# Linear attention with a SwiGLU gate on one core: the w_phi load laid out by partition, four weight folds ahead of x's transposes, and the first two tiles of x normalised one by one

## Chip, cores and metric

The kernel runs on one core of one Trainium2 chip. The metric is device time in microseconds, the median of three runs. The opening of the kernel, the first 70 us or so, is what the change edits; the rest stays as it is.

## What is computed

x is 2048 rows by 1024 columns. It is layer-normalised to xn. From xn comes a gate (SwiGLU with 3584 hidden columns, then a Silu) and an attention value s: 32 heads of width 32, whose queries and keys go through a small matrix of their head, w_phi, and a softmax of the result and of its negative.

```
xn = layernorm(x)
q, k, v = split(xn @ wqkv)                       # 32 heads, width 32
phi(a) = [softmax(a @ w_phi[h]), softmax(-a @ w_phi[h])]
o = phi(q) (phi(k)^T v) / (phi(q) sum(phi(k)) + 1e-6)
s = o @ wo
g = silu((silu(xn @ w1) * (xn @ w3)) @ w2)
out = x + s * g
```

## The kernel before

Products are made in a Strassen-like form: a 2 x 2 block product takes seven block products instead of eight, with sums of blocks as operands (A11, A12, S1, S2, S3, S4 and A22 of x; B11, B21, T1 to T4 and B22 of the weights). Each operand is split by `split` (L91 to L94) into a rounded high part (a cast on ScalarE, L93) and a remainder (a subtraction on VectorE, L94), and each block product takes three passes of TensorE over these parts (L627). w_phi is not multiplied with queries and keys; it is folded into the weights beforehand: `fold` (L244 to L249) multiplies a transposed block of wk or wq with `bd`, a block-diagonal matrix made of w_phi by GpSimd (L293 to L296). There are 32 folds; 22 are made in the opening by `first_folds` (L306 to L314), 10 later, one by one, beside the main loop. A fold loads `wr` (256 KB, L241), runs eight matmuls into a PSUM tile `pw` (L248), is copied back over `wr` by ScalarE (L312), and is stored to DRAM (L313). All loads and stores here go through SP's one queue.

Two sets of buffers matter. `wr` comes from a pool `work` of five buffers (tag "w"), which block 0's weight sum `t2` shares in the opening. The PSUM tiles `pt` of the transposes (`turn`, L216 to L220) and `pw` of the folds share three buffers (tag "tr"); each is emptied by a copy on ScalarE (L224 or L312).

The opening (L275 to L361): load w_phi (L276), tiles 0 to 3 of x, the weights of block 0 of w1 and w3 (`rw`, L257), four fold blocks (L241), tiles 4 to 7 of x, the weights of block 1. Tiles 0 to 3 give A11 and A12, tiles 4 to 7 A21 and A22. For a tile, `stats` (L192 to L196) makes mean and variance on VectorE; `rstd` (L198 to L209) makes the reciprocal root for a pair of tiles, one square root on ScalarE (L202) and five small operations on VectorE (L203 to L208); `norm` (L211 to L214) normalises the two halves of a tile in place. Then come the transposes, copies and splits of A11 for the four tiles, two folds, those of A12, the splits of two operands of block 1, the statistics of tiles 4 to 7, and three folds. Then each of tiles 4 to 7 is turned, the sums S1 to S4 are made by VectorE (`a_sums`, L227 to L237) and two folds follow each tile; the last three operands are split with three folds after each. GpSimd sums block 0's weights (`b_sums`, L129 and L130) before the first of these.

A scheduler orders the instructions of each engine in this part, by program order and by when it takes their inputs to be ready. The main loop's first four products, (block 0: A11, A12; block 1: A11, A12), may be mixed with the opening; from step 4 on the order of the five engines is the program's (L616), and 56 blocks of seven products follow, with side work hung on their steps. Later phases make keys and values, queries, w2, and the output.

Of the kernel before, what the change touches and what calls it, by code (L numbers as in the profile page):

```python
# [8 lines left out]
F = mybir.dt.float32  # L9
# [7 lines left out]
S, D, H, DH, FF = 2048, 1024, 32, 32, 3584  # L17
P = 128
# [3 lines left out]
G = 8  # L22
# [6 lines left out]
def tile_kernel(ctx: ExitStack, tc: tile.TileContext, x, wkT, wqT, wv, wphi, wo, w1, w3, w2, out):  # L29
    nc = tc.nc  # L30
    open_pools = {}

    def pool(name, bufs, **kw):

        open_pools[name] = tc.tile_pool(name=name, bufs=bufs, reuse_waits="tile", **kw)
        return open_pools[name].__enter__()
# [101 lines left out]
    small = pool("small", 2)  # L138
    work = pool("work", 5)
# [14 lines left out]
    def slot(m, j):  # L154
        name = f"op{m}" + (ANAMES if m < 2 else BNAMES)[j]
        j = HOMES[m][j]
        if j < 7:
            return big.tile([P, 2, 4, 512], R, name=name, tag=f"big{j}")
        return spare.tile([P, 2, 4, 512], R, name=name, tag=f"spare{j}")
# [12 lines left out]
    def quad(name, dt=R):  # L172
        return qp.tile([P, 2, 4, P], dt, name=name, tag="q")

    def blk(name):
        return xp.tile([P, 4, P], F, name=name, tag="x")

    def flat(t):
        return t.rearrange("p k t -> p (k t)")
# [7 lines left out]
    def load_x(t, halves):  # L187
        for h in range(2):
            nc.sync.dma_start(halves[h], x[t * P:(t + 1) * P, h * 512:(h + 1) * 512])
        return halves  # L190

    def stats(mv, j, xt):  # L192
        st = small.tile([P, 2, 6], F, name="st")
        for a in range(2):
            nc.vector.bn_stats(st[:, a, :], xt[a])
        nc.vector.bn_aggr(mv[:, j], st.rearrange("p a b -> p (a b)"))  # L196

    def rstd(mv):  # L198

        sd = small.tile([P, 4, 2], F, name="sd")  # L200
        var = mv[:, :, 1]
        nc.scalar.activation(sd[:, 0], var, AF.Sqrt, bias=eps_t)  # L202
        nc.vector.reciprocal(sd[:, 1], sd[:, 0])  # L203

        nc.vector.tensor_mul(sd[:, 2], sd[:, 1], sd[:, 1])
        nc.vector.scalar_tensor_tensor(sd[:, 3], var, EPS, sd[:, 2], op0=OP.add, op1=OP.mult)
        nc.vector.tensor_scalar(sd[:, 3], sd[:, 3], -0.5, 1.5, op0=OP.mult, op1=OP.add)
        nc.vector.tensor_mul(sd[:, 1], sd[:, 1], sd[:, 3])  # L208
        return sd  # L209

    def norm(mv, sd, j, xt):  # L211

        for a in range(2):
            nc.vector.tensor_scalar(xt[a], xt[a], mv[:, j, 0:1], sd[:, 1, j:j + 1], op0=OP.subtract, op1=OP.mult)  # L214

    def turn(half):  # L216
# [22 lines left out]
    def load_w(wT, dch, c, t=None):  # L239
        wr = blk("wr") if t is None else t  # L240
        nc.sync.dma_start(wr, wT[dch][:, 4 * c:4 * c + 4])  # L241
        return wr

    def fold(wr, c):  # L244

        pw = ps.tile([P, 4, P], F, name="pw", tag="tr", bufs=3)
        for g in range(4):
            nc.tensor.matmul(pw[:, g, :], wr[:, g], bd[:, 4 * c + g, :], start=True, stop=True)  # L248
        return pw  # L249

    folds = [(wkT, k, c, wk_d[c][k]) for c in range(2) for k in range(ND)]
    folds += [(wqT, k, c, wq_d[c][k]) for c in range(2) for k in range(ND)]

    def b_load(f, rw, n):

        a, h = {"B11": (0, 0), "B21": (0, 1), "B12": (1, 0), "B22": (1, 1)}[n]
        nc.sync.dma_start(rw[:, a, h], (w1, w3)[a][f][:, 4 * h:4 * h + 4].rearrange("p k n -> p (k n)"))  # L257
# [15 lines left out]


    phi_raw = flat(blk("phi")[:, :2]).rearrange("p (g f) -> p g f", f=DH)  # L275
    nc.sync.dma_start(phi_raw, wphi.rearrange("(g p) f -> p g f", p=P))  # L276
    ao, bo, bo1, xs = {n: slot(0, j) for j, n in enumerate(ANAMES)}, {}, {}, []
    rws = [rwp.tile([P, 2, 2, 512], F, name="rw", tag="rw") for _ in range(2)]
    for t in range(8):
        if t in (4, 5):  # L280
            xs.append(load_x(t, [flat(blk("xt")) for _ in range(2)]))
        else:
            r = quad("xt", F).rearrange("p u k t -> p u (k t)")
            xs.append(load_x(t, [r[:, 0], r[:, 1]]))
        if t == 3:
            for n in ("B11", "B22", "B12", "B21"):
                b_load(0, rws[0], n)
            early_w = [load_w(*folds[k][:3], work.tile([P, 4, P], F, name="wr", tag="w")) for k in range(4)]
    for n in ("B11", "B21", "B22", "B12"):
        b_load(1, rws[1], n)  # L290
    make_identity(nc, ident)
# [14 lines left out]
    def first_folds(n):  # L306
        nonlocal at_fold
        for _ in range(n):
            wT, k, c, d = folds[at_fold]
            wr = early_w.pop(0) if early_w else load_w(wT, k, c, work.tile([P, 4, P], F, name="wr", tag="w"))  # L310
            pw = fold(wr, c)
            nc.scalar.copy(wr, pw)  # L312
            nc.sync.dma_start(d, flat(wr))  # L313
            at_fold += 1  # L314

    mvs = [small.tile([P, 2, 2], F, name="mv", bufs=4) for _ in range(4)]
    raw = [{} for _ in range(4)]
    for t in range(4):
        stats(mvs[t // 2], t % 2, xs[t])
    for p in range(2):  # L320
        sd = rstd(mvs[p])
        for j in range(2):
            norm(mvs[p], sd, j, xs[2 * p + j])
    for q in range(4):
        raw[q]["A11"] = raw_x(turn(xs[q][0]))
        first_split("A11", q, raw[q]["A11"])
        if q == 1:
            next(b_gen)
    first_folds(2)
    for q in range(4):  # L330
        raw[q]["A12"] = raw_x(turn(xs[q][1]))
        first_split("A12", q, raw[q]["A12"])
# [4 lines left out]
        split(bo1[n][:, 0], bo1[n][:, 1], rws[1][:, 0, h].rearrange("p (k n) -> p k n", n=P))  # L337
    for q in range(4):
        stats(mvs[2 + q // 2], q % 2, xs[4 + q])
    first_folds(3)  # L340
    next(b_gen)
    for q in range(4):
        if q % 2 == 0:
            sd = rstd(mvs[2 + q // 2])
            for j in range(2):
                norm(mvs[2 + q // 2], sd, j, xs[4 + q + j])
        raw[q]["A21"] = raw_x(turn(xs[4 + q][0]))
        raw[q]["A22"] = raw_x(turn(xs[4 + q][1]))
        a_sums(raw[q], nc.vector)
        first_split("S2", q, raw[q]["S2"])  # L350
        first_split("S1", q, raw[q]["S1"])
        if q == 2:
            next(b_gen)
        first_folds(2)
# [58 lines left out]
    def side_x(i, s0):  # L413
# [9 lines left out]
        for j in range(2):  # L423
            at_ = room(at_ + 1, 1.6)
            at(at_, lambda j=j: stats(mv[0], j, xt[j]))
        at_ = room(at_ + 1, 1.0)
        at(at_, lambda: sd.append(rstd(mv[0])))
        for j in range(2):
            at_ = room(at_ + 1, 1.0)
            at(at_, lambda j=j: norm(mv[0], sd[0], j, xt[j]))  # L430
# [183 lines left out]
    for step, (k, an) in enumerate(seq):  # L614
        if step == 4:
            in_order(ENG.PE, ENG.Activation, ENG.DVE, ENG.Pool, ENG.SP)  # L616
        tb, f = divmod(k, NF)
# [475 lines left out]
    for r, new in enumerate(steps):  # L1093
# [31 lines left out]
        if 26 <= r < 34:  # L1125
            c, a = (r - 26) // 4, (r - 26) % 4
            nc.sync.dma_start(zr_d[32 * a:32 * a + 32, c], z_d[:, c, a].rearrange("o j s f -> o (j s f)").to_broadcast([32, 256]))
        if 8 <= r < 24:
            c, j, s = (r - 8) // 8, (r - 8) // 2 % 4, r % 2
# [64 lines left out]
    halves = [(b, a, c) for b in range(NB) for a in range(2) for c in range(2)]  # L1194
# [121 lines left out]
```

## Time and profile before

| | |
|---|---|
| median of three runs | 2379.27 us (2379.09 to 2381.4) |
| the profiled execution | 2381.26 us |
| its span | 2379.0 us |
| TensorE, VectorE, ScalarE, GpSimd busy | 98%, 75%, 36%, 32% |
| first transposes on TensorE | 13.65 us |
| last fold of the opening on TensorE | 70.02 us |

In the profile, PE is TensorE, PEld its weight loads, DVE VectorE, ACT ScalarE, POOL GpSimd and SP the engine that issues DMAs. A timeline row has a start in us, a duration in us, the engine, the line, the operation, output and inputs by their names with shapes, a count of instructions that were merged, and in brackets how long the engine had been idle before and what ended that. A windows row has the stretch and its length, then the busy time of PE, PEld, DVE, ACT and POOL with counts of instructions, the clock that TensorE was granted (1.00 is full), the busy share of the DMA engines, and GB/s. A row of the chain has a start, a duration and what the chain went through. A row of a group has a line, what it does and its count, then the busy time in us and the mean in ns, then the idle time before it and its cause. SPq is SP issuing a DMA.

### The profile page before, as it was taken

Reading aid. Unit: us, or ns where it says so; the run is one execution under the profiler, and the core shown is the slowest. Engines: PE = TensorE matmul, PEld = TensorE weight load, DVE = VectorE, ACT = ScalarE, POOL = GpSimd, SP = SyncE. Lnnn points to the kernel's source line nnn. Section 1 sums busy time; section 2 is a strip of 40 time slices with the busy share of each in tenths; the row PEclk is TensorE's granted clock in tenths of the full one; section 3 lists DMA queues with packets and bytes.
Section 4 is the critical chain, followed back from the end, with each engine's and each line's share of the span. In section 5 each row is a group of like instructions: output and inputs, shape, how many; then the busy total and the mean of one; then the engine's idle time right before and its main releaser. Section 6 shows DMA issues by size and latency. Waiting matters only on the chain.

```text
span 2379.0 us, 35819 instructions
## 1 busy us (share of the span) xinstructions
PE 2339.5 (98%) x13298; PEld 1923.9 (81%) x13298; DVE 1773.7 (75%) x2511; ACT 856.1 (36%) x1506; POOL 762.1 (32%) x569
## 2 busy tenths in 40 slices
PE   6999999999999999999999999999999999999999
PEld 5788888888888888888888787887888888887777
DVE  8567788775688878884575565787678788888993
ACT  6445544443345544453221111234422222242010
POOL 1333555552355555552000000230011111115872
PEclk9999999999999999999999999999999999999999
DMA  7667789877887787776998867998434443277653
GB/s 262 200 218 238 232 288 312 288 246 230 260 272 257 250 280 274 262 268 232 364 345 334 321 215 292 348 352 295 152 123 163 177 182 135 99 274 285 229 190 121
DMA packets 319406, 586.83 MB, mean 247 GB/s; under 512 B 25600, under 2 KB 158208, under 8 KB 316544
## 3 DMA queue, kind: packets, MB, share of 16 engines
q1 hardware_dynamic: 304448, 569.87, 69.3%
q10 hardware_dynamic: 14784, 14.68, 1.8%
q8 instruction: 105, 1.72, 0.3%
q14 instruction: 69, 0.57, 0.1%
HBM read 379.19 MB, written 205.79 MB: 246 GB/s over the span
## 4 chain that ended last, share of the span: by engine, by line
PE 90%; DVE 4%; DMA 3%; issue 1%; ACT 1%; POOL 0%; SPq 0%; ACTq 0%; POOLq 0%; DVEq 0%
PE bankb L627 25%; PE bankc L627 12%; PE bankb L1074 11%; PE bankb L679 10%; PE pm L1190 7%; PE banka L627 6%; PE bankc L1074 6%; PE bankc L679 5%; PE banka L1074 3%; PE banka L679 2%; PE po L1048 1%; PE pkv L665 1%; PE pw L248 1%; DMA hr<-h_d 1%; DMA e_d<-eq 0%
## 5 line engine op out<-in xcount | busy, mean ns | idle before, releaser
L94 DVE TENSOR_TENSOR bo<-rw,bo 128x512 fp32r<-128x512 f32 x336 | 311.7, 928 | 151.5 <-ACT bo L93 148.5
L1084 POOL TENSOR_TENSOR acc<-acc,u 128x512 f32<-128x512 f32 x48 | 64.4, 1342 | 455.5 <-ACT u L1083 440.8
L93 ACT CAST bo<-rw 128x512 fp32r<-128x512 f32 x336 | 201.1, 617 | 4.0 <-DMA w_d0T<-w2o 2.0
L1074 PE MATMUL bankb<-bo,as 128*128 128x512 f32 x816 | 201.1, 389 | 0.4 <-DVE acc L1086 0.4
L1074 PEld LDWEIGHTS bankb<-bo,as 128*128 128x128 f32 x816 | 153.1, 188 | 32.6 <-DVE acc L1086 0.8
L1190 PE MATMUL pm<-wos,oT 128*128 128x512 f32 x720 | 168.7, 393 | 3.6 <-DVE gx L1209 3.6
L627 PE MATMUL bankb<-op0A,bo 128*128 128x512 f32 x672 | 164.0, 391 | 0.0
L1190 PEld LDWEIGHTS pm<-wos,oT 128*128 128x128 f32 x720 | 135.6, 189 | 34.9 <-DVE gx L1209 4.0
L627 PE MATMUL bankb<-op0S,bo 128*128 128x512 f32 x672 | 163.0, 391 | 0.0
L627 PE MATMUL bankc<-op0S,bo 128*128 128x512 f32 x672 | 162.9, 391 | 0.0
L627 PE MATMUL bankc<-op1S,bo 128*128 128x512 f32 x672 | 161.5, 389 | 1.2 <-ACT bo L93 1.2
L627 PE MATMUL bankb<-op1A,bo 128*128 128x512 f32 x672 | 161.4, 389 | 0.0
L627 PE MATMUL bankb<-op1S,bo 128*128 128x512 f32 x672 | 161.4, 389 | 0.0
L627 PEld LDWEIGHTS bankc<-op1S,bo 128*128 128x128 f32 x672 | 126.0, 188 | 27.7 <-ACT bo L93 1.6
L1074 PE MATMUL bankc<-bo,as 128*128 128x512 f32 x576 | 146.6, 389 | 1.1 <-ACT as L93 0.7
L627 PEld LDWEIGHTS bankb<-op1S,bo 128*128 128x128 f32 x672 | 126.1, 188 | 26.2
L627 PEld LDWEIGHTS bankb<-op1A,bo 128*128 128x128 f32 x672 | 126.1, 188 | 26.2
L627 PEld LDWEIGHTS bankc<-op0S,bo 128*128 128x128 f32 x672 | 125.5, 188 | 25.7
L627 PEld LDWEIGHTS bankb<-op0A,bo 128*128 128x128 f32 x672 | 125.4, 188 | 25.7 <-DVE op0A L94 0.2
L627 PEld LDWEIGHTS bankb<-op0S,bo 128*128 128x128 f32 x672 | 125.4, 188 | 25.6
L1074 PEld LDWEIGHTS bankc<-bo,as 128*128 128x128 f32 x576 | 108.0, 188 | 24.3 <-ACT as L93 1.1
L129 POOL TENSOR_TENSOR rw<-rw 128x512 f32<-128x512 f32 x56 | 82.5, 1474 | 135.3 <-DMA rw<-in_w 119.2
(245 smaller groups left out, 4723.1 us busy)
## 6 DMA issues: line engine op xcount, KB each, us to landing
rw<-in_w SPq DMA_DIRECT2D x224, 256.0 KB, 3.5
hr<-h_d SPq DMA_DIRECT2D x56, 512.0 KB, 3.9
xoS<-xo_d0S SPq DMA_DIRECT2D x48, 512.0 KB, 8.7
xoS<-xo_d1S SPq DMA_DIRECT2D x48, 512.0 KB, 7.0
xoA<-xo_d0A SPq DMA_DIRECT2D x36, 512.0 KB, 7.8
xoA<-xo_d1A SPq DMA_DIRECT2D x36, 512.0 KB, 6.1
e<-e_d SPq DMA_DIRECT2D x32, 512.0 KB, 6.1
h_d<-h SPq DMA_DIRECT2D x56, 256.0 KB, 4.3
```

The costliest lines, as they stand in the source:

```text
L93: nc.scalar.copy(hi, src)
L94: (by or nc.vector).tensor_sub(lo, src, hi.bitcast(F))
L129: nc.gpsimd.tensor_sub(b12, b22, b12)
L248: nc.tensor.matmul(pw[:, g, :], wr[:, g], bd[:, 4 * c + g, :], start=True, stop=True)
L627: nc.tensor.matmul(bank, bt[:, w, kk], aos[tb][an][:, u, kk], start=an in ("A11", "A12", "S1") and n == 0, stop=LAST[b] == an and n == 11, ...
L665: nc.tensor.matmul(pkv[sl, m], e[:, m // 4, (m % 4) * P + 32 * h:(m % 4) * P + 32 * h + 32], v[:, 4 * (m % 4) + h], start=first and m == 0 ...
L679: nc.tensor.matmul(bank[b], xo[an][:, u, k], wb[bn][:, w, k], start=an in ("A11", "A12", "S1") and n == 0, stop=LAST[b] == an and n == 11, ...
L1048: nc.tensor.matmul(po[a][32 * j:32 * j + 32, 256 * c:256 * c + 256], kvt[sl, c, j, s], ets[c, j // 2][sl, 2 * (j % 2) + s].rearrange("p t ...
L1074: nc.tensor.matmul(bank[b], t[:, u, pos + k], bos[kb, bn, k][:, w], start=first and n == 0, stop=LAST[b] == an and n == 5, skip_group_chec ...
L1084: nc.gpsimd.tensor_add(c, c, u)
L1190: nc.tensor.matmul(p, oT[a][k // 4][:, u, k % 4], wos[c, 4 * (k % 2) + k // 2][:, w], start=n == 0, stop=n == 23)
```

## The change

w_phi is handed over in the layout of the SBUF tile, so that each partition reads one run of 1 KB; before, it read eight runs of 128 B. The four fold blocks that are loaded early are loaded ahead of block 0's weights. Tiles 0 and 1 of x are normalised one at a time, each with its own rstd, so there are three rstds for the first four tiles instead of two. Tiles 2 and 3 share one, and their first halves are normalised before their second halves. Four folds stand right behind tiles 0 and 1, ahead of the other tiles' statistics and of all transposes; the two folds between A11 and A12 are gone, and one stands where three stood. The opening still makes 22 folds.

```diff
-        sd = small.tile([P, 4, 2], F, name="sd")
+        sd = small.tile([P, 4, 2], F, name="sd", bufs=4)[:, :, :mv.shape[1]]
...
-    def norm(mv, sd, j, xt):
-
-        for a in range(2):
+    def norm(mv, sd, j, xt, *halves):
+
+        for a in halves or range(2):
             nc.vector.tensor_scalar(xt[a], xt[a], mv[:, j, 0:1], sd[:, 1, j:j + 1], op0=OP.subtract, op1=OP.mult)
...
-    nc.sync.dma_start(phi_raw, wphi.rearrange("(g p) f -> p g f", p=P))
+    nc.sync.dma_start(phi_raw.rearrange("p g f -> p (g f)"), wphi)
...
         if t == 3:
+            early_w = [load_w(*folds[k][:3], work.tile([P, 4, P], F, name="wr", tag="w")) for k in range(4)]
             for n in ("B11", "B22", "B12", "B21"):
                 b_load(0, rws[0], n)
-            early_w = [load_w(*folds[k][:3], work.tile([P, 4, P], F, name="wr", tag="w")) for k in range(4)]
...
-    for t in range(4):
-        stats(mvs[t // 2], t % 2, xs[t])
-    for p in range(2):
-        sd = rstd(mvs[p])
-        for j in range(2):
-            norm(mvs[p], sd, j, xs[2 * p + j])
+    for t in range(2):
+        stats(mvs[0], t, xs[t])
+        one = mvs[0][:, t:t + 1]
+        norm(one, rstd(one), 0, xs[t])
+    first_folds(4)
+    for t in range(2):
+        stats(mvs[1], t, xs[2 + t])
+    sd = rstd(mvs[1])
+    for a in range(2):
+        for t in range(2):
+            norm(mvs[1], sd, t, xs[2 + t], a)
...
-    first_folds(2)
     for q in range(4):
         raw[q]["A12"] = raw_x(turn(xs[q][1]))
...
-    first_folds(3)
+    first_folds(1)
...
-        "wphi": np.asarray(A_w_phi).reshape(H * DH, DH),
+        "wphi": np.asarray(A_w_phi).reshape(G, P, DH).transpose(1, 0, 2).reshape(P, G * DH),
```

## Prediction

> **What bounds the kernel now.** The page comes first: TensorE is busy nearly all of the span, and the chain that ended last is 90% TensorE.
>
> ```profile
> span 2379.0 us, 35819 instructions
> PE 2339.5 (98%) x13298; PEld 1923.9 (81%) x13298; DVE 1773.7 (75%) x2511; ACT 856.1 (36%) x1506; POOL 762.1 (32%) x569
> PE 90%; DVE 4%; DMA 3%; issue 1%; ACT 1%; POOL 0%; SPq 0%; ACTq 0%; POOLq 0%; DVEq 0%
> ```
>
> So a change to the opening can only win time in which TensorE does nothing there, and what it wins stays won if TensorE is dense afterwards. The windows view gives the opening by stage (busy time of each engine in ten microseconds).
>
> ```profile
> 0.00:10.00 10.00, 0.00 (x0) 0.00 (x0) 3.51 (x8) 1.58 (x2) 3.17 (x11) 1.00 0.77 251
> 10.00:20.00 10.00, 3.92 (x16) 2.88 (x17) 9.69 (x25) 3.07 (x7) 2.59 (x2) 1.00 1.04 390
> 20.00:30.00 10.00, 10.00 (x61) 9.26 (x60) 10.00 (x20) 8.82 (x18) 4.60 (x3) 1.00 0.59 212
> 30.00:40.00 10.00, 9.90 (x61) 8.19 (x60) 9.63 (x27) 9.12 (x19) 0.00 (x0) 1.00 0.63 210
> 40.00:50.00 10.00, 9.10 (x70) 8.01 (x68) 10.00 (x18) 9.11 (x19) 0.00 (x0) 1.00 0.69 236
> 50.00:60.00 10.00, 7.55 (x49) 5.85 (x47) 7.55 (x13) 8.73 (x17) 0.00 (x0) 1.00 0.87 269
> 60.00:70.00 10.00, 8.07 (x49) 6.54 (x50) 7.49 (x12) 5.15 (x10) 4.17 (x3) 1.00 0.86 277
> ```
>
> TensorE idles 16.1 us of the first 20, then 0.1, 0.9, 2.45 and 1.93 us per stage: 21.5 us in all. But from 10 to 50 VectorE is full and from 20 to 50 ScalarE is at nine tenths, so emptying TensorE there need not bring the end forward. The chain in order of time says what held which stretch.
>
> ```profile
> 2.33 5.71 DMA xt<-in_x
> ...
> 46.71 3.88 DMA wr<-in_wkT
> ...
> 55.36 3.14 DMA wk_d<-wr
> ...
> 65.19 4.70 DMA wr<-in_wqT
> ...
> 71.15 1.16 PE bankc L627 x5
> ```
>
> First the loads of x, then VectorE, and from about 43 us the folds: load, fold, copy, store, and only then is the buffer free for the next load. TensorE runs dense from 71.15. The question is how much earlier that moment comes.
>
> **Part 1: w_phi by partition.** The old view reads runs of 32 floats; the new one reads one run of 1 KB per partition.
>
> ```profile
> 2.00:3.40 1.40, 0.00 (x0) 0.00 (x0) 0.00 (x0) 0.01 (x1) 0.22 (x2) 1.00 1.04 221
> 8.10:10.00 1.90, 0.00 (x0) 0.00 (x0) 1.87 (x4) 0.30 (x1) 0.00 (x0) 1.00 1.05 402
> ```
>
> The DMA engines are as busy in the first stretch (share 1.04) as in the second (1.05), yet move 221 GB/s against 402: 0.31 MB where 0.56 MB would have gone, that is 0.25 MB, or 0.6 us at 402. The loads of x queue behind it on SP's one queue. Bounds: nothing, if SP's pace of issuing them is what counts, to the 1.4 us of the stretch. I take 0.6.
>
> **Part 2: the order of the loads.** SP issues in program order here.
>
> ```profile
> 1.24 3.89 SPq L189 DMA_DIRECT2D xt<-in_x  x8
> 5.17 3.85 SPq L257 DMA_DIRECT2D rw<-in_w  x4
> 9.30 2.31 SPq L241 DMA_DIRECT2D wr<-in_wkT  x4
> ...
> 24.88 1.95 SPq L241 DMA_DIRECT2D wr<-in_wkT  x2
> ...
> 42.94 0.33 SPq L241 DMA_DIRECT2D wr<-in_wkT  x1
> ```
>
> The four fold loads go from 9.30 to 5.17, block 0's weights behind them, so that GpSimd's sums of these weights come later by the 2.31 us that four issues took. Nobody waits for the sums soon: in the program the first use of these weights, the split of B11, stands behind the second tile's transposes, and those of the first tile run at 13.65 (row below). The cost is nothing but a collision, priced below.
>
> **Part 3: the first two tiles one by one.** VectorE's work up to the eighth norm, row by row.
>
> ```profile
> 4.71 1.34 DVE L195 BATCH_NORM_STATS2 st<-xt 128x6 f32<-128x512 f32 x2 [3.84 <-DMA xt<-in_x]
> 8.06 1.34 DVE L195 BATCH_NORM_STATS2 st<-xt 128x6 f32<-128x512 f32 x2 [1.77 <-DMA xt<-in_x]
> 9.56 1.23 DVE L195 BATCH_NORM_STATS2 st<-xt 128x6 f32<-128x512 f32 x2
> 12.73 0.29 ACT L202 ACTIVATE sd<-mv,consts 128x2 f32<-128x2 f32 x1 [2.76 <-DVE sd L207]
> 12.96 3.82 DVE L214 TENSOR_SCALAR xt<-xt,mv,sd 128x512 f32<-128x512 f32 x4
> 13.37 1.27 POOL L129 TENSOR_TENSOR rw<-rw 128x512 f32<-128x512 f32 x1 [8.33 <-DMA rw<-in_w]
> 13.65 1.09 PE L219 MATMUL pt<-ident,xt 128*128 128x128 f32 x4 [13.65 <-DVE xt L214]
> 14.72 1.32 POOL L130 TENSOR_TENSOR t<-rw 128x512 f32<-128x512 f32 x1
> 16.70 0.15 DVE L203 RECIPROCAL sd<-sd 128x2 f32<-128x2 f32 x1
> 17.69 1.92 DVE L214 TENSOR_SCALAR xt<-xt,mv,sd 128x512 f32<-128x512 f32 x4
> ```
>
> Before, the eight norms are done at 17.69 + 1.92 = 19.61, after a hole of 1.77 us in which VectorE waits for the second tile. Prices: a tile's statistics 1.50 (8.06 to 9.56), an rstd 0.99 (16.70 to 17.69), a norm of half a tile 0.48 (1.92 over four), the wait for ScalarE's square root about 0.4 (an estimate: the 0.29 of its row and the handing over). After, from x's landing at 4.71 - 0.6 = 4.1: 4 x 1.50 + 3 x 0.99 (one more than before) + 8 x 0.48 + 0.4 = 13.2, hence 17.3. The second tile is wanted at 4.1 + 1.50 + 0.4 + 0.99 + 0.96 = 7.95 and lands at 8.06 - 0.6 = 7.46: the hole is filled. The 0.99 of the added rstd has that hole as its cover; without it, it is lost in full. The waits for the other two square roots can be covered by other tiles' statistics; if not, they add up to 0.8.
>
> Then the collision. Four norms took 3.82 us while GpSimd ran L129 and L130, and 1.92 us without it: 1.90 us. After, these two sums start at about 13.37 + 2.31 - 0.6 = 15.1 and last 2.7 us, and the last four norms would run from 15.4 to 17.3: again wholly beside them. I take the full 1.90: eight norms done at 19.2, a gain of 0.4 us. Bounds: -0.4 (collision and both waits) to 2.3 (neither). The Trainium skill, SBUF — State Buffer, Who interferes with whom, speaks against the change at this place: such a VectorE operation and a GpSimd operation exclude each other for a whole instruction, so that four separate norms can be stopped each time. By that rule the time lost is as before; had the trace shown no slowing, the eight norms would be done at 17.3.
>
> **Part 4: four folds first.** The next rows are what the folds cost and where they stand.
>
> ```profile
> L312 ACT COPY wr<-pw 128x512 f32<-128x512 f32 x22 | 12.9, 592 | 9.6 <-PE pw L248 9.6
> ```
>
> ```profile
> 32.40 0.50 ACT L202 ACTIVATE sd<-mv,consts 128x2 f32<-128x2 f32 x2
> 35.08 0.69 DVE L571 TENSOR_TENSOR h<-banka,h 128x512 f32<-128x512 f32 x1
> 35.67 2.82 DVE L214 TENSOR_SCALAR xt<-xt,mv,sd 128x512 f32<-128x512 f32 x6
> 36.01 1.28 ACT L572 ACT_TABLE_LOAD   x1
> 36.36 1.08 PE L219 MATMUL pt<-ident,xt 128*128 128x128 f32 x8
> 37.28 1.06 PE L248 MATMUL pw<-bd,wr 128*128 128x128 f32 x8
> 37.84 1.05 ACT L224 COPY xf<-pt 128x512 f32<-128x512 f32 x2
> ```
>
> A fold is eight matmuls, 1.06 us, and a copy of 0.59 us. Four of them, 4.2 us of TensorE and 2.4 us of ScalarE, leave the stretch 20 to 32 us for the empty one before 14. Who waits for it: the transposes stand behind these folds on TensorE. Issued at 5.17, with the 3.85 us that four issues then took and the 5.71 us from issue to landing of the chain's first row, less 0.6, the last one lands at about 9.0 + 5.7 - 0.6 = 14.1; the first transposes then start at about 15 instead of 13.65. By then two tiles are normalised and their four halves follow without a gap, and VectorE, which is the one that is full, has statistics and norms until 19: this costs nothing, at most 1.4 us if a split of A11 is what VectorE lacks.
>
> What does the lead bring? The folds after these four keep their places in the program: one ahead of the second group's transposes, two behind each tile of it, then three after each of the last operands. In the trace TensorE ran transposes and folds in program order throughout. Sixth fold: loaded with the pair issued at 24.88 (over at 26.83), in place some 4 us later (the load at 46.71 took 3.88), but run at 37.28, right behind the transposes of 36.36, which wait for the norms of 35.67. It lay ready for over 6 us. So the sixth and later folds move only as those norms do, by VectorE's 0.4 us, and the buffers' rounds with them: from 42.94 to 65.19 twelve loads, 2.02 us apart, five buffers, 10.1 us a round, in loads and stores that the change does not touch.
>
> Beyond the 0.4 us: at 36.36 ScalarE is late. The first four transposes are over near 36.9, but their copy runs at 37.84, behind a table load and a Silu. With 2.4 us of copies gone ahead of it, up to 0.9 us is won here; I take 0.9, since ScalarE is at nine tenths from 20 on. After it, VectorE waits 2.45 us between 50 and 60, mostly for ScalarE; what can be won there lies between 0 and 2.45, and I take 0.7, near the lower end, since in that stage ScalarE waits for folds (9.6 us in the row of L312).
>
> **Sum.** 0.4 + 0.9 + 0.7 = 2.0 us less. The profiled execution took 2381.26 us (span 2379.0 and 2.3 around it), so 2379.3 for it; the median of the runs is 2379.27, 2.0 below the profiled one, hence **2377.3**. Differences under 0.2%, 4.8 us, a measurement of this kernel can hardly tell from none.
>
> **Rivals.** *The folds keep their lead.* If the scheduler lets the sixth to eighth folds, whose buffers are then loaded well before 30 us, run ahead of the second group's transposes, the rounds start three folds earlier: 3 x 2.02 = 6.1 us, 2373.2. For it: TensorE waits at 50 to 70 for folds; ScalarE has 9.6 us of such waits. Against it: the sixth fold that lay ready. Chance 0.25.
>
> *The square roots fall behind the Silu.* Before, both square roots of the second group (32.40) stand ahead of the first Silu, so one table load (36.01, 1.28 us) is enough. With the folds off TensorE, block 0's second product can be ready before 32.40 rather than just before the add at 35.08; a Silu scheduled then makes ScalarE change tables twice more: 2.6 us in a stretch where it has no room, and VectorE's norms of 35.67 wait for it. From the point where that product is done more than 2.7 us earlier than now it decides; the four folds are 4.2 us of TensorE. It takes the 0.9 and 0.7 too: 2379.3 - 0.4 + 2.6 = 2381.5. Chance 0.12.
>
> *Nothing comes through.* The wr loads land late, the transposes start after 15 us, the collision and both square roots are paid (-0.4), and the rounds of the folds take what is left: 2379.3. Chance 0.13.
>
> **The numbers.** The forecast holds 0.50; its own range is 2375.0 (the terms at 2.3, 0.9 and 1.1) to 2379.7 (-0.4 and nothing else). For 8 in 10 the range reaches to the first rival and most of the second: 2371.5 to 2381.0. Faster by over 0.2%: the first rival and a little of the forecast's tail, 0.27; slower by over 0.2%: only the second rival with its waits doubled, 0.06; the rest, 0.67, lies between.
>
> **What would show it.** Right: x's first statistics near 4.1; the four folds on TensorE before any transpose; the eighth norm near 19 with norms slowed beside L129 and L130; the second group's first transposes near 36, the sixth fold right behind them; the first dense bank group near 69 instead of 71.15. Wrong: folds six to eight ahead of the transposes and dense work from 65; or more than two table loads on ScalarE before 55 us; or an idle VectorE between 10 and 30.

## The result, and the profile after

The changed kernel takes 2404.1 us (median of 4 runs, 2403.37 to 2406.54); the kernel before, in the same comparison, 2379.49 us (2379.09 to 2381.4). The ratio is 1.0104, 95% interval 1.0092 to 1.0116: 24.6 us slower, where 2.0 us less was forecast and the range ended at 2381.0. The profiled execution took 2406.54 us. Its page begins:

```profile
span 2404.5 us, 35834 instructions
PE 2363.2 (98%) x13298; PEld 1926.0 (80%) x13298; DVE 1770.0 (74%) x2516; ACT 857.4 (36%) x1507; POOL 760.4 (32%) x569
```

The span is 25.5 us longer, with the same 13298 matmuls; and TensorE's busy time is 23.7 us longer. A loss by waiting would show as idle time. This one shows mostly as matmuls that take longer, so the first question is which. The view of one line's instructions gives for each shape the count, the duration in ns (smallest, median, largest), and when the first and the last started. First the kernel before:

```profile
L627 PE MATMUL bankb<-op0A,bo x672: 387/389/499, 24.5 to 613.7; 128*128 128x512 f32 x168
L627 PE MATMUL bankb<-op1S,bo x672: 389/389/389, 608.4 to 1134.7; 128*128 128x512 f32 x168
L627 PE MATMUL banka<-op1A,bo x336: 389/389/389, 603.0 to 1121.1; 128*128 128x512 f32 x168
L679 PE MATMUL bankb<-op2T,xoS x192: 389/389/497, 1145.8 to 1299.7; 128*128 128x512 f32 x192
L1074 PE MATMUL bankb<-bo,as x816: 387/389/497, 1634.8 to 2174.4; 128*128 128x512 f32 x164
```

Then the changed kernel, whose lines stand four further down:

```profile
L631 PE MATMUL bankb<-op0A,bo x672: 387/389/497, 23.4 to 621.1; 128*128 128x512 f32 x168
L631 PE MATMUL bankb<-op1S,bo x672: 388/389/499, 615.8 to 1147.3; 128*128 128x512 f32 x168
L631 PE MATMUL banka<-op1A,bo x336: 394/394/394, 608.7 to 1133.6; 128*128 128x512 f32 x168
L683 PE MATMUL bankb<-op2T,xoS x192: 388/394/501, 1158.4 to 1313.8; 128*128 128x512 f32 x192
L683 PE MATMUL bankb<-op4T,xoS x192: 388/389/467, 1495.5 to 1641.1; 128*128 128x512 f32 x192
L1078 PE MATMUL bankb<-bo,as x816: 387/394/398, 1649.7 to 2197.8; 128*128 128x512 f32 x164
```

Read the starts first. The last fold of the opening runs 4.7 us late (74.72 against 70.02, rows below), and the first products with operands op1, near 600, 5.7 us (608.7 against 603.0 for banka). By 1650 it is 14.9 us (1649.7 against 1634.8), at the last product of that group 23.4 us. So two losses stand one behind the other, and the larger is nowhere near the edited code.

Now the durations of the 128x512 matmuls. Most take 389 ns as before, but all 336 with banka and op1A take 394, and so does the median of op2T's and of the last phase's. They do not share a phase, for op1S runs in the same one at 389. They share a place. The program lays its pools into a partition of SBUF from two ends: the small tiles, the five `wr` buffers, the weight operands `bo` and seven large operand slots from the left, and from the right the raw weights and the x blocks; the place of the x blocks is later taken by two more operand slots, and then by tiles of the late phases. Where the program's text names the place, the slow matmuls have one operand in each end (A11 and A12 of op1 lie in the right-hand slots); op0's, op1S's and op4's operands lie all in the left end and stay at 389. One group of 96 does not fit (bankb from op3T and xoA, both in the left end): its median is 393 here and 389 in e2 below.

A matmul's duration is not yet its price, since the next one starts before it ends: twelve of 389 ns would add up to 4.7 us, and they take 2.88. What counts is the time of such a row of twelve, first before, then after:

```profile
602.99 2.88 PE L627 MATMUL banka<-op1A,bo 128*128 128x512 f32 x12
```

```profile
608.65 2.96 PE L631 MATMUL banka<-op1A,bo 128*128 128x512 f32 x12
```

That is 0.08 us for twelve, 6.7 ns for each. Counted over the whole trace, 3389 of the 128x512 matmuls take 392 to 399 ns in the changed kernel and 294 before. The 3095 more, at 6.7 ns, come to 20.7 us.

What moved the ends against each other is two words of the first line in the diff: `sd` got bufs=4 in place of 2. An `sd` is 8 floats per partition, 32 bytes; two more push everything behind it in the left end up by 64 bytes, and nothing in the right end.

The opening itself, in the timeline of the changed kernel:

```profile
4.19 0.69 DVE L195 BATCH_NORM_STATS2 st<-xt 128x6 f32<-128x512 f32 x1 [3.33 <-DMA xt<-in_x]
11.03 6.68 PE L248 MATMUL pw<-bd,wr 128*128 128x128 f32 x32 [11.03 <-DMA wr<-in_wkT]
14.42 3.82 DVE L214 TENSOR_SCALAR xt<-xt,mv,sd 128x512 f32<-128x512 f32 x4
14.96 1.59 POOL L129 TENSOR_TENSOR rw<-rw 128x512 f32<-128x512 f32 x1 [10.34 <-DMA rw<-in_w]
16.62 1.33 POOL L130 TENSOR_TENSOR t<-rw 128x512 f32<-128x512 f32 x1
17.55 2.47 PE L219 MATMUL pt<-ident,xt 128*128 128x128 f32 x20
...
37.99 1.92 DVE L214 TENSOR_SCALAR xt<-xt,mv,sd 128x512 f32<-128x512 f32 x4
39.17 1.04 PE L219 MATMUL pt<-ident,xt 128*128 128x128 f32 x8
40.05 1.95 PE L248 MATMUL pw<-bd,wr 128*128 128x128 f32 x16
...
59.93 1.13 PE L248 MATMUL pw<-bd,wr 128*128 128x128 f32 x8 [2.81 <-DMA wr<-in_wkT]
63.70 2.05 PE L248 MATMUL pw<-bd,wr 128*128 128x128 f32 x8 [2.64 <-DMA wr<-in_wqT]
...
74.72 1.13 PE L248 MATMUL pw<-bd,wr 128*128 128x128 f32 x8 [0.26 <-DMA wr<-in_wqT]
```

It starts as forecast. x's first statistics run at 4.19, four folds come before any transpose, and the eighth norm ends at 14.42 + 3.82 = 18.24 instead of 19.61. Then the lead is lost: the second group's norms run at 37.99, where they ran at 35.67; TensorE waits 2.81 and 2.64 us for the loads of two folds near 60; and the last fold runs at 74.72 instead of 70.02. Near 60 SP issues in bunches: three loads from 50.89, three stores from 54.55, and no load again until 60.52, where before it issued them singly, mostly by turns. One row stands out: the eight matmuls at 63.70 take 2.05 us, those at 59.93 take 1.13. By the view of the line in these stretches one matmul takes 421 ns there and 275 ns here:

```profile
L248 PE MATMUL pw<-bd,wr x28: 344/421/553, 11.0 to 16.9; 128*128 128x128 f32 x28
L248 PE MATMUL pw<-bd,wr x8: 275/275/347, 59.9 to 60.8; 128*128 128x128 f32 x8
L248 PE MATMUL pw<-bd,wr x8: 421/421/552, 63.7 to 65.3; 128*128 128x128 f32 x8
```

The first of the three rows is that of the four folds at the front; they, too, ran at 421. So did the first folds of the kernel before, whose row is:

```profile
L248 PE MATMUL pw<-bd,wr x16: 421/421/421, 20.2 to 23.4; 128*128 128x128 f32 x16
```

The windows view of the changed kernel says what happened at 63.70 (the column behind POOL's is the granted clock):

```profile
30.00:40.00 10.00, 9.37 (x42) 7.81 (x43) 8.71 (x25) 5.92 (x12) 0.03 (x1) 0.83 0.46 150
...
60.00:70.00 10.00, 7.36 (x38) 6.58 (x39) 6.72 (x11) 4.74 (x9) 0.00 (x0) 0.66 0.60 213
...
62.00:68.00 6.00, 4.30 (x14) 3.85 (x15) 5.72 (x10) 3.43 (x7) 0.00 (x0) 0.50 0.85 304
```

Before, the clock was 1.00 in every such stage. Now it is 0.50 from 62 to 68, so that TensorE, when its fold is there at last, takes 2.05 us over it instead of 1.13. In the two ten-microsecond rows the busy time at the missing share of the clock comes to 9.37 x 0.17 + 7.36 x 0.34 = 4.1 us, an estimate of what the low clock costs TensorE; how much of it reaches the end the experiments below have to tell. The Trainium skill, TensorE: Matmul & The Clock Gate, Part 1: The HAM clock gate, says that about 3.4 us without work halve the clock and that about as long of steady work restores it. The trace agrees in the kind and not in the length: the clock is 0.50 behind waits of which the longest is 2.81 us. The first work of a kernel should by the same rule be slow; at the front the clock column shows 1.00, but the 421 ns of the matmuls are those of the half clock.

### The profile page after: what moved, and what is told of

Same layout as the page of the kernel before. It is cut to its first block, busy times and chain, and to the rows that moved or that the text cites. A ratio compares the mean times of both kernels' runs of the same rounds, so it can differ in the third digit from the quotient of the medians.

```text
span 2404.5 us, 35834 instructions
## 1 busy us (share of the span) xinstructions
PE 2363.2 (98%) x13298; PEld 1926.0 (80%) x13298; DVE 1770.0 (74%) x2516; ACT 857.4 (36%) x1507; POOL 760.4 (32%) x569
```

## Experiments on the late loss: 64 bytes

Theory A: the 64 bytes cost the late loss, through the addresses of the operands. Its rival, B: the loss has to do with the opening's order or with the buffers themselves. `small` begins with an unused tile of PAD floats, so that the left end can be moved by itself.

**e1_addr_back**: the changed kernel with the 64 bytes taken out of the pad.

```diff
-PAD = 32
+PAD = 16
```

> The changed kernel with the pad tile of the small pool cut from 32 to 16 floats, so that the 64 bytes per partition which two more sd buffers added are taken out again and every later tile on that side has its old address; the order of all engines' instructions is the changed kernel's. Theory A (two causes: some 7 to 8 us are lost in the opening, and some 17 us later because operand tiles moved by 64 bytes and matmuls from about 600 us on take 394 ns instead of 389): about 2387, with 389 ns as the median of the L1078 matmuls. Theory B (one cause, the new order of the opening, which drags the later phases along): about 2404, with 394 ns as now.

Measured: 2382.67 us (10 runs), ratio to the kernel before 1.0015 (1.0005 to 1.0024). The row that was slow:

```profile
L1078 PE MATMUL bankb<-bo,as x816: 388/389/499, 1637.4 to 2176.8; 128*128 128x512 f32 x164
```

389 ns again, and 21.4 of the 24.6 us are gone. What is left, 3.1 us, is the opening.

**e2_addr_only**: the reverse, the kernel before with 64 bytes put in and nothing else.

```diff
-PAD = 32
+PAD = 48
```

> The kernel before with the pad tile made 64 bytes larger and nothing else, the order of all instructions as before. Theory A: slower by about 17 us, some 2396, with the opening as before (first dense bank group at 71 us) and the L1074 matmuls at 394 ns. Theory B: no difference, 2379.

Measured: 2400.19 us (4 runs), ratio 1.0087 (1.0072 to 1.0102).

```profile
L1074 PE MATMUL bankb<-bo,as x816: 387/394/398, 1645.2 to 2192.2; 128*128 128x512 f32 x164
```

Nothing of the change is in this kernel, and it loses 20.6 us. A holds, though it had put the late loss at 17 us; B falls for the late loss.

**e5_both_sides** and **e6_right_only**: is it the position of the left end, or that of one end against the other (theory C)? The right end begins with an unused tile too. e5 moves both ends by 64 bytes, e6 the right one alone.

```diff
-PAD = 32
+PAD = 48
...
-    edge[1].tile([P, 120], F, name="edge_r")
+    edge[1].tile([P, 104], F, name="edge_r")
```

e6 has the second of these edits only.

> The kernel before with the tiles of both ends of the memory moved up by 64 bytes: the pad 64 bytes larger on the left, the edge tile 64 bytes smaller on the right. Theory C (what counts is how the two operands of a matmul lie to each other, modulo some power of two: the slow ones read one from the left end and one from the right): both moved alike, so 2379 again and 389 ns throughout. Theory D (what counts is each operand's own alignment, here to 128 bytes or more): as slow as with the left moved alone, 2400, or slower.

> The kernel before with the right end alone moved up by 64 bytes. Theory C: as slow as with the left moved alone, about 2400, with 394 ns for the products that read the spare tiles on the right (A12 of the second half, T1 of the third operand set) and 389 for those that read left tiles only. Theory D with the left operand as the one that matters: 2379.

Measured: e5 2380.84 us (10 runs), ratio 1.0006 (0.9997 to 1.0015), no loss; e6 2394.38 us (2 runs), ratio 1.0063 (1.0043 to 1.0084). Both ends moved together cost nothing, either alone costs: the relative position decides. But e6 is not e2 again. Its loss is 14 us, and its rows mix 387 to 398 ns:

```profile
L1074 PE MATMUL bankb<-bo,as x816: 387/392/398, 1639.4 to 2184.7; 128*128 128x512 f32 x164
```

**e11_left_128** and **e14_right_along** followed later: another distance, and the changed kernel mended at the other end.

```diff
-PAD = 32
+PAD = 64
```

> The kernel before with its left end moved up by 128 bytes instead of 64 (PAD 32 to 64), the right end where it was. If any difference of the two ends costs the same, late matmuls with operands from both ends take 394 ns and the time is about 2400 us, as with 64 bytes. If only the position modulo 128 bytes counts, they take 389 ns and the time is about 2380 us. A value in between, say 391 ns and 2390 us, would speak for a cost that depends on the distance.

Measured: 2399.04 us (5 runs), ratio 1.0080 (1.0067 to 1.0094). 128 bytes cost about as much as 64, though again by a mixture:

```profile
L1074 PE MATMUL bankb<-bo,as x816: 387/392/399, 1642.8 to 2189.8; 128*128 128x512 f32 x164
```

So 128 bytes is not a step that would make the ends agree. Three displacements were run and all three cost; no larger one was.

```diff
-    edge[1].tile([P, 120], F, name="edge_r")
+    edge[1].tile([P, 104], F, name="edge_r")
```

> The changed kernel with its right end moved by the same 64 bytes as the left one (edge_r 120 to 104 floats), no byte taken out of the left end. If the relative position of the two ends costs the 21 us, they go: about 2382.7 us, late matmuls back at 389 ns. If it were the two extra buffers themselves, the time stays at about 2404 us.

Measured: 2384.17 us (11 runs), ratio 1.0017 (1.0009 to 1.0026), with all that the change adds, the two buffers included.

```profile
L1078 PE MATMUL bankb<-bo,as x816: 388/389/628, 1636.9 to 2177.8; 128*128 128x512 f32 x164
```

Hence the two buffers cost nothing as buffers. Their 64 bytes, on one side only, cost the difference of the ratios, 1.0104 less 1.0015 to 1.0017: 0.0087 to 0.0089, about 21 us, which is what the 3095 slower matmuls came to above. In the traces of e1 and e14 the matmuls of 392 to 399 ns are down to 317 and 292.

What in the chip makes them slower, no run shows. The Trainium skill, TensorE: Matmul & The Clock Gate, Part 2, Step-by-step: what each phase is for, gives TensorE two independent read ports into SBUF, so that loading the next weights takes nothing from the running matmul. By that the place of the operands should not matter; here it does, by 394 against 389 ns.

## Experiments on the opening

From here the 64 bytes are taken out (PAD = 16), so that only the opening speaks.

**e3_folds_back** and **e4_phi_only**: e3 keeps the layout of w_phi, the order of the loads and the norms one by one, and puts the folds back to two and three; e4 is the kernel before with the layout alone.

```diff
-    first_folds(4)
...
+    first_folds(2)
...
-    first_folds(1)
+    first_folds(3)
```

> The changed kernel with the old addresses (pad 16) and the folds where they were before: two between A11 and A12, three ahead of the second group. The w_phi layout, the order of the loads and the norms one by one stay. If the loss in the opening comes from the four folds at the front (TensorE left with gaps after them, SP held at the load that waits for the buffer of block 0's sum): about 2379, within 1 us of before, dense at about 70 us. If it comes from the norms one by one (a third rstd) or the order of the loads: about 2386, as much as in the run with the old addresses alone.

> The kernel before with the w_phi layout alone. As predicted in the sum: x's first statistics about 0.6 us earlier, and 0 to 0.6 us off the time, 2379. If SP's pace of issuing is what counts: the first statistics at 4.7 us as before and no difference at all. A time above 2381 would make this part a cause of the loss, which neither theory expects.

Measured: e3 2377.95 us (10 runs), ratio 0.9994 (0.9985 to 1.0004); e4 2378.91 us (10 runs), ratio 0.9999 (0.9990 to 1.0009). Neither can be told from no change. e3 against e1 tells the cost of the four folds at the front: 0.9994 against 1.0015, 0.0021 or 5 us, and the intervals just do not touch. In e3's trace the clock is 1.00 in every stage from 20 to 80 us, no wait of TensorE there is over 1.4 us, and the last fold runs at 67.10:

```profile
67.10 1.05 PE L248 MATMUL pw<-bd,wr 128*128 128x128 f32 x8
```

What makes TensorE wait longer with four folds at the front? The waits of SP's queue name a candidate in the changed kernel (who waits for whom, us in total, times, longest):

```profile
SPq L241 <- DVE bo L94: 6.9, 1, 6.9
```

The ninth load of a fold needs the buffer of `t2`, block 0's weight sum, and SP stands for it 6.9 us, everything behind it too. **e7_t2_apart** gives `t2` a buffer of its own in e1, **e8_back_t2_apart** does the same in e3.

```diff
-        t2 = work.tile([P, 512], F, name="t2", tag="w")
+        t2 = work.tile([P, 512], F, name="t2", tag="h1", bufs=2)
```

> The changed kernel with the old addresses, and block 0's weight sum t2 in another pool slot (the one that the main loop's first evictions use later), so that the folds have all five buffers from the start. The order of SP's queue is the same. If the 3 us that the opening lost come from SP standing 6.9 us at the load that waits for t2's buffer: that wait is gone, the folds' rounds start some 5 us earlier, and the time falls to 2378 to 2379. If they come from TensorE's gaps after the folds were taken out of them (it is granted half the clock at 31 to 35 and 62 to 68 us): 2382 to 2383 still.

> The run with the folds back in their old places, old addresses, w_phi by partition, loads in the new order and norms one by one, and t2 in the other slot as well. If t2's buffer holds the folds' rounds here too: 2 to 4 us below the run with the folds back, 2374 to 2376. If the rounds of 10 us that all five buffers go through are the limit from 43 us on, whatever comes first: no difference, 2378.

Measured: e7 2382.93 us (10 runs), ratio 1.0014 (1.0005 to 1.0024), no better than e1; e8 2380.44 us (10 runs), ratio 1.0005 (0.9995 to 1.0014). With SP free the wait only moves:

```profile
60.41 1.85 PE L248 MATMUL pw<-bd,wr 128*128 128x128 f32 x8 [3.59 <-DMA wr<-in_wqT]
```

It is 3.59 us, and the eight matmuls behind it again take 1.85. The candidate falls.

**e9_two_first** divides the four: two folds at the front, two between A11 and A12.

```diff
-    first_folds(4)
+    first_folds(2)
...
+    first_folds(2)
```

> The changed kernel with the old addresses, two folds at the front and two between A11 and A12 (four and none in the change). If it is the number of folds taken out of the gaps between the transposes that costs time (TensorE idle at 20 to 30 us): half of the loss against the run with the folds back, about 2380. If it is the order that SP's queue gets (here again loads in threes and fours and stores in threes, as with four in front): no gain, 2382 to 2383.

Measured: 2381.36 us (10 runs), ratio 1.0009 (1.0000 to 1.0018): between e1 and e3, and not to be told from either.

**e12_act_store** (in e1) and **e13_back_act_store** (in e3) let ScalarE issue the stores of the folds, so that loads no longer stand behind stores in SP's queue.

```diff
-            nc.sync.dma_start(d, flat(wr))
+            nc.scalar.dma_start(d, flat(wr))
```

> The changed kernel with the old addresses, and the stores of the opening's folds issued by ScalarE, right behind the copy that makes them, instead of by SP. SP's queue then holds loads alone. If stores that wait for ScalarE hold up the loads behind them on SP (the wait of the seventeenth fold for its load): that wait is gone or under 1 us, dense work starts at 66 to 68 us, and the time is 2377 to 2379. If the rounds of load, fold, copy and store are the limit whichever queue issues: within 1 us of 2382.7. The scheduler orders the engines anew here, so a third of a gain could come from that.

> The same for the run with the folds back in their old places (old addresses, the rest of the change kept): stores from ScalarE. If SP's mixed queue limits that order as well: 2 to 4 us under the run with the folds back, 2374 to 2376, below the kernel before. If not: 2378.

Measured: e12 2384.76 us (6 runs), ratio 1.0029 (1.0017 to 1.0041); e13 2390.69 us (4 runs), ratio 1.0052 (1.0037 to 1.0067). Both are slower, e13 by half a per cent. The queue shared by loads and stores is not shown to be the cause; but the scheduler arranges the engines anew here, so this edit is no clean test.

**e10_warm** goes for the clock itself. In e1, eleven products of `ident` with itself go into the PSUM tile of the seventeenth fold, ahead of the fold, which then overwrites them. They do nothing but keep TensorE at work in the wait. (The trace shows each of these products as two matmuls, 22 in all, as it shows the four of a fold as eight.)

```diff
+        [nc.tensor.matmul(pw[:, g % 4, :], ident, ident, start=True, stop=True) for g in range(warm)]
...
-            pw = fold(wr, c)
+            pw = fold(wr, c, 11 if at_fold == 16 else 0)
```

> The changed kernel with the old addresses, and eleven matmuls of the identity by itself (about 2.4 us) put on TensorE just ahead of the seventeenth fold, into the tile that this fold then overwrites: TensorE stood idle there for 2.9 us waiting for a load. Order and waits of everything else are unchanged. If the half clock that TensorE was granted at 61 to 68 us is what the wait costs: the granted clock stays at 1.00 there and the time falls by 2 to 3 us, to about 2380. If the wait itself is the cost and the clock does nothing: 2382.7 as without, or more.

Measured: 2379.99 us (10 runs), ratio 1.0003 (0.9994 to 1.0013). First the timeline of e1, then that of e10:

```profile
57.63 1.13 PE L248 MATMUL pw<-bd,wr 128*128 128x128 f32 x8 [0.63 <-DMA wr<-in_wkT]
61.70 2.05 PE L248 MATMUL pw<-bd,wr 128*128 128x128 f32 x8 [2.93 <-DMA wr<-in_wqT]
...
73.61 1.13 PE L248 MATMUL pw<-bd,wr 128*128 128x128 f32 x8 [0.46 <-ACT wk L578]
```

```profile
55.51 1.13 PE L248 MATMUL pw<-bd,wr 128*128 128x128 f32 x8 [0.60 <-DMA wr<-in_wkT]
56.47 2.62 PE L246 MATMUL pw<-ident 128*128 128x128 f32 x22
59.31 1.16 PE L248 MATMUL pw<-bd,wr 128*128 128x128 f32 x8 [0.22 <-DMA wr<-in_wqT]
...
69.59 1.13 PE L248 MATMUL pw<-bd,wr 128*128 128x128 f32 x8 [0.23 <-ACT wk L578]
```

The load of the seventeenth fold keeps TensorE until 59.31, but the wait is filled, its eight matmuls take 1.16 us, and the last fold runs 4.0 us earlier. Of these 4.0 us, 2.1 were there before the filling: the sixteenth fold already runs at 55.51 instead of 57.63. The windows of e1 from 60 to 68, then those of e10:

```profile
60.00:64.00 4.00, 2.31 (x10) 2.24 (x11) 4.00 (x7) 2.72 (x6) 0.00 (x0) 0.61 0.88 291
64.00:68.00 4.00, 4.00 (x16) 3.42 (x15) 2.69 (x5) 0.41 (x1) 0.00 (x0) 0.53 0.56 209
```

```profile
60.00:64.00 4.00, 4.00 (x28) 3.30 (x26) 4.00 (x8) 1.59 (x3) 0.00 (x0) 1.00 0.85 215
64.00:68.00 4.00, 3.03 (x22) 2.83 (x22) 0.56 (x1) 1.76 (x3) 0.86 (x1) 1.00 0.69 255
```

**e15_warm_late** is the control: the same eleven one fold later, behind the wait (`at_fold == 17`). **e16_warm_both** puts eleven ahead of the fifth and of the seventeenth fold (`at_fold in (4, 16)`).

> The changed kernel with the position mended, and the eleven matmuls one fold later, so that they stand behind TensorE's wait of about 2.9 us and not in it. If the half clock after the wait is what costs, they help nothing: the clock is near 0.5 at 62 to 66 again and the time is 2382.7 us or up to 3 us more, as the eleven themselves then run late and at half clock. If the eleven help by something else than the clock (another order of the queues), the time is about 2380 us here too.

> The same eleven matmuls ahead of the fifth and ahead of the seventeenth fold. If the earlier low clock at 30 to 36 costs on the path too, the time falls below that of the seventeenth alone (2380.0 us), to about 2378.5 us; if the earlier one is hidden beside the waits for the loads and VectorE, it stays at 2380 us. The eleven ahead of the fifth may themselves stand in the way, up to 2 us.

Measured: e15 2384.22 us (11 runs), ratio 1.0019 (1.0010 to 1.0027); e16 2383.38 us (9 runs), ratio 1.0017 (1.0008 to 1.0027). The rows of e15:

```profile
61.16 2.05 PE L248 MATMUL pw<-bd,wr 128*128 128x128 f32 x8 [3.71 <-DMA wr<-in_wqT]
```

```profile
60.00:64.00 4.00, 2.84 (x13) 2.87 (x14) 4.00 (x7) 1.81 (x4) 0.00 (x0) 0.50 0.89 301
```

Behind the wait the same matmuls help nothing: the clock is 0.50 and the loss is there. So it is not their presence that helped in e10 but that they fill the wait. By the ratios the half clock costs 0.0012 to 0.0014 (e1 and e14 against e10), about 3 us; e15's 0.0016 has the eleven's own time at half clock in it. e10's interval overlaps those of e1, e14 and e15 a little. The granted clock that stands on record for each execution speaks for the same cause: its mean is 0.9980 over e10's ten runs, 0.9966 over e1's, 0.9971 over e14's and 0.9965 over e15's. From e10 to e1 that is 0.0014, or 3.3 us of 2380, and from e10 to e14 0.0009, or 2.1 us.

The traces, one execution each, do not show where these 3 us are lost. e14's runs almost level with e10's up to the sixteenth fold (55.64 and 55.51), and then has a wait of 2.73 us and a fold at half clock behind it:

```profile
55.64 1.13 PE L248 MATMUL pw<-bd,wr 128*128 128x128 f32 x8 [0.69 <-ACT wr L312]
59.50 1.99 PE L248 MATMUL pw<-bd,wr 128*128 128x128 f32 x8 [2.73 <-DMA wr<-in_wqT]
...
70.09 1.13 PE L248 MATMUL pw<-bd,wr 128*128 128x128 f32 x8 [0.32 <-DMA wr<-in_wqT]
```

Its last fold runs only 0.5 us behind e10's 69.59. That the half clock near 60 costs 3 us on the path is therefore supported by the medians and the clocks, and not shown.

e16 missed. Its fold's wait moved ahead of the filling (2.07 us before 57.81) and the clock fell there in spite of it:

```profile
57.81 2.05 PE L248 MATMUL pw<-bd,wr 128*128 128x128 f32 x8 [2.07 <-DMA wr<-in_wkT]
59.65 4.39 PE L246 MATMUL pw<-ident 128*128 128x128 f32 x22
```

The wait before that one was 1.66 us, with one fold between. So e16 says nothing on what the earlier low clock, between 20 and 36, costs. In e1 the clock is 0.83 from 30 to 40; in e10, e14 and e15 it is 0.83 from 20 to 30 and 1.00 after. Nothing in e14 against the changed kernel touches the opening, so where the clock drops there is a matter of the execution, and this part is left open. The length of a wait alone does not decide either: in e13 the clock stayed at 1.00 behind a wait of 2.82 us (at 61.54), and in e2, which has the folds of the kernel before, it was 0.57 from 56 to 60 behind waits of 1.31 and 0.78 us.

## Why the prediction was wrong

The forecast of 2377.3 us and its range missed by far. The steps, in the order of the prediction:

- **w_phi by partition.** x's first statistics run at 4.19 (4.1 forecast). In e4 they run at 4.38, and as time it is nothing that can be measured (0.9999, 0.9990 to 1.0009).
- **The norms and the collision.** GpSimd's two sums ran beside the last four norms, which took 3.82 us, twice the 1.92 they take alone, so the full price was right. The eighth norm ended at 18.24, a gain of 1.4 us instead of 0.4, since the last four norms began at 14.42 and not at 15.4: what stands ahead of them (statistics, three rstds, the wait for a square root) was priced 1 us too high.
- **Four folds first, "this costs nothing, at most 1.4 us".** This step failed. The first fold began at 11.03 and the last of the four loads landed at 12.9 (about 14.1 said), but the folds took 6.68 us, not 4.2: they were priced with the 1.06 us of a fold at 37.28, and as TensorE's first work they ran at 421 ns a matmul instead of 275. The trace of before had the right price, in its first two folds: 16 matmuls at 421 ns, in the stretch from 20.2 to 23.4. The first transposes came at 17.55 instead of about 15, 3.9 us after the 13.65 of before, where at most 1.4 was allowed for. e3 puts the whole of the four folds at 5 us.
- **The rounds of the folds "in loads and stores that the change does not touch".** This failed with it. The sixth fold did lie right behind the transposes, as said, but these ran at 39.17 and not near 36, and near 60, where SP's loads and stores now come in bunches, TensorE had two long waits. The prediction treated a wait of TensorE as its own length; by e1, e10 and e14 it seems to cost the clock afterwards too, about 3 us here.
- **ScalarE's late copy, 0.9, and VectorE's waits, 0.7.** Neither came: the copy that ran at 37.84 was to be earlier and its transposes now run 2.8 us later.
- **The buffers of `sd`.** This term is missing from the sum altogether, and it is 21 of the 24.6 us. The diff that the prediction worked from shows bufs=4; the prediction priced each instruction that was added or moved, and gave a tile that got more buffers no price at all. No row of before shows the effect, since all late matmuls took 389 ns there, but a bound could have been written: what it costs if every address behind `small` moves.

None of the rivals was the mechanism. The one that ended on the slower side (square roots behind the Silu) did not take place either: ScalarE still has one table load between 2 and 55 us, at 36.08. Of the right forecasts the signs at the start of the opening were the best, and they were true of a stretch that did not decide.

Two things stay open: why four folds at the front lengthen the waits near 60 (neither `t2`'s buffer nor, as far as e12 goes, the shared queue explains it; the bunches on SP are not tested by themselves), and whether the last 2 us between e10 and e3 are real, since their intervals overlap.

## What to carry to other kernels

Read a diff for its bytes as well as for its instructions: a small tile that gets more buffers moves all that is laid out behind it, and a compute-bound kernel whose operands lie in pools at both ends can lose by it, here 0.9%. When an edit changes a small pool, look at the median duration of one unchanged matmul far from the edit; if it differs, restore the relative position with a pad before judging the edit. And when work is moved ahead out of a stretch, ask whether it was what kept TensorE busy there: a wait of about 3 us can be paid a second time, in the clock after it.

## What was not expected of the hardware

- The same 128x512 matmul takes 389 ns or 394 ns, by where one operand lies against the other, and twelve in a row take 0.08 us longer. Moving the left end by 64 bytes against the right one gave mostly 394 in the affected groups, 64 bytes of the right end or 128 of the left gave a mixture up to 398 ns, and 64 bytes of both gave 389. The whole kernel follows with ratios of 1.0087, 1.0063, 1.0080 and 1.0006.
- The granted clock fell to 0.50 behind waits of 2.6 to 3.7 us, and the eight matmuls of a fold then took 1.85 to 2.05 us instead of 1.13. In e16 waits of 1.66 and 2.07 us were enough, in e2 1.31 and 0.78, while in e13 the clock stayed at 1.00 behind 2.82.
- TensorE's first work after 11 us without any ran at 421 ns a 128x128 matmul until about 17 us, and in the kernel before, where it began at 13.65, still from 20.2 to 23.4. The same matmul later takes 275, although the profile's clock column shows 1.00 there.
